# Attention into soft MoE on one core: routing matmuls moved to another place of the turn, a row pitch of 72, a shared beacon setup

## The chip, the cores and the metric

The kernel runs on one core of a Trainium2 chip. The metric is device time in microseconds (us) of one execution, smaller being better. Executions of this kernel scatter more than its profile suggests: 43 runs of the unchanged kernel on one chip lay between 235.8 and 248.6 us. A run is called fast when it is within 1.5% of the fastest run of the same kernel, else slow. With one core there is no second die to compare with, and the scatter turned out to be continuous, so beside the ratio of fast runs I give medians or means over all runs of the same rounds where they matter, and say which is which. A verdict (faster, same, slower at 2%, or unclear) rests on fast runs alone.

## The reference, cut to what matters

```python
# q, k, v: (8, 8, 576, 64); beacon_k, beacon_v: (8, 8, 16, 64)
k_all = np.concatenate([beacon_k, k], axis=2)
v_all = np.concatenate([beacon_v, v], axis=2)
a = softmax(causal(scale * q @ k_all.T))          # shortened
x = (a @ v_all).transpose(0, 2, 1, 3).reshape(4608, 512)
logits = x @ phi                                   # 32 slots
d = softmax(logits, axis=0); c = softmax(logits, axis=1)
slot_input = d.T @ x
slot_out = relu(slot_input @ w1[e]) @ w2[e]        # 8 experts, 4 slots each
out = c @ slot_out
```

## The kernel before

A turn n of the main loop scores one pair of heads and attends the pair before it. Four steps of scores go through two PSUM tiles, sc0 and sc1. Transposes and routing matmuls share two PSUM buffers of the tag tr; there is no third one.

```python
ps_tr = ctx.enter_context(tc.tile_pool(name="ps_tr", bufs=2, space=PSUM))
vh = [const.tile([P, NCH, H, DD], F16, name=f"vh{i}") for i in range(2)]   # DD = 65
...
def logit_piece(b):
    lp = ps_tr.tile([P, NCH, NSL], FP, name="tr", tag="tr")
    ...                                            # 20 matmuls xT x phi
    nc.scalar.activation(dT[b][:, :, :], lp[:, :, :], AF.Exp)
    nc.vector.memset(dT[b][0:Nb, 0, :], 0.0)
...                                                # el_piece, si_piece: 20 matmuls each, too
for n in range(NP + 1):
    score(n, 0)
    if n >= 2:
        xt_piece(n - 2)          # x^T: one tr buffer, copied out by VectorE
    score(n, 1)
    transp(n + 1)                # q, then k: two tr buffers, copied out by VectorE
    ...
    if n >= 5:                   # logits, eL, slot inputs, or nothing: one tr buffer
        br, gr = divmod(n - 5, H // 2)
        (logit_piece, el_piece, si_piece, lambda b_: None)[gr](br)
    attend(n - 1, 0)
    score(n, 2)
    attend(n - 1, 1)
    score(n, 3)
    load_pair(n + 5)
    ...                          # V of the next batch: load, cast
    while wl < min(24, (n - 3) * 2 // 3):
        load_w(wl)               # a half of an expert's weights, on POOL's queue
        wl += 1
```

The softmax here doesn't subtract the row's maximum and nothing guards it: scores larger than these inputs give would overflow.

## Time and profile before

| | before |
|---|---|
| median of three runs | 240.89 us (240.24 to 241.42) |
| span of the profile | 233.8 us |
| busy: PE, DVE, ACT, POOL | 71%, 60%, 52%, 38% |
| loop, from the first exponential of turn 5 to that of turn 31 | 34.30 to 161.75 us |
| last weight load landed | 204.33 us |
| DMA row (busy share of the 16 DMA engines) | nine tenths or more from 6 to 140 us |

The profile fell on a quick execution: 235.7 us, while the timed ones were at 241. I return to what this hid. The length of a turn is read from the timeline, as the distance of the first exponentials (128x1024) of two turns.

### The profile page before, as it was taken

The numbers are of one execution on the slowest core, as the hardware profiler recorded it, in microseconds if no ns is written. First come the engines' busy times: TensorE is split into PE (matmuls) and PEld (weight loads), VectorE is DVE, ScalarE is ACT, GpSimd is POOL, SyncE is SP. The second block draws the span as 40 slices with busy tenths as digits, with TensorE's granted clock in tenths as the row PEclk, the third lists the DMA queues.
The fourth block names the chain that finished last, engine by engine and source line by source line (L and its number), as shares of the span: only waits on it lengthen the run. The fifth ranks groups of instructions, "written<-read, shape, count | busy, mean of one in ns | idle before, by whom it ended". The sixth has DMA issues, their size and how long they took to land.

```text
span 233.8 us, 8459 instructions
## 1 busy us (share of the span) xinstructions
PE 165.9 (71%) x3728; PEld 119.0 (51%) x3728; DVE 139.1 (60%) x303; ACT 122.7 (52%) x164; POOL 87.7 (38%) x162
## 2 busy tenths in 40 slices
PE   0579988887878888788777878888589530488400
PEld 0457766666666666666555666666455310223100
DVE  4575786876767777788564778866572000059700
ACT  2085687677757668758564875877201000059600
POOL 5082444654346363565334436535824200000000
PEclk9999999999979999999997999999955555559955
DMA  6999999999999999999999996537799999829996
GB/s 212 229 297 282 296 238 268 282 250 197 265 298 266 268 248 217 263 307 250 229 256 281 263 279 114 98 47 123 110 195 207 211 207 209 143 111 424 409 422 251
DMA packets 63716, 55.66 MB, mean 238 GB/s; under 512 B 41920, under 2 KB 50112, under 8 KB 62656
## 3 DMA queue, kind: packets, MB, share of 16 engines
q1 hardware_dynamic: 50880, 38.35, 57.2%
q0 software_dynamic: 12800, 16.78, 42.4%
q8 instruction: 29, 0.48, 0.9%
q14 instruction: 7, 0.06, 0.1%
HBM read 62.46 MB, written 9.44 MB: 308 GB/s over the span
## 4 chain that ended last, share of the span: by engine, by line
PE 46%; DVE 18%; DMA 11%; ACT 10%; issue 5%; SPq 4%; POOL 0%; DVEq 0%; POOLq 0%
DMA w2h<-in_moe_w_dram 9%; ACT ex L206 7%; PE sc_154 L200 7%; PE tr L185 6%; PE av_150 L227 6%; PE tr L253 6%; PE sc_155 L200 5%; PE fp L407 3%; DVE qT_129 L187 3%; DVE qT_130 L187 3%; DVE xb_141 L235 3%; DVE qT_128 L187 3%; SPq L103 2%; PE tr L371 2%; PE av_151 L227 2%
## 5 line engine op out<-in xcount | busy, mean ns | idle before, releaser
L206 ACT ACTIVATE ex<-sc_154 128x1024 f16<-128x1024 f32 x64 | 62.9, 983 | 46.8 <-PE sc_154 L200 46.7
L208 POOL TENSOR_SCALAR_AFFINE_SELECT ex<-ex 128x1024 f16<-128x1024 f16 x32 | 34.8, 1088 | 80.3 <-ACT ex L206 80.3
L206 ACT ACTIVATE ex<-sc_155 128x992 f16<-128x992 f32 x64 | 48.2, 753 | 2.3 <-PE sc_155 L200 2.3
L227 PEld LDWEIGHTS <-ex 128*128 128x128 f16 (+2 forms) x960 | 38.6, 110 | 8.6 <-issue 7.5
L257 DVE COPY xT<-tr 128x592 f16<-128x592 f16 x32 | 14.9, 466 | 12.8 <-PE tr L253 12.8
L371 PE MATMUL tr<-siT,w1h 128*128 128x4 f16 x256 | 8.2, 167 | 13.8 <-DMA w1h<-in_moe_w_dram 13.0
L185 PE MATMUL tr<-idb,qf 64*64 64x64 bf16 x576 | 16.3, 202 | 1.5 <-PE sc_155 L200 0.8
L185 PE MATMUL tr<-idb,kf 64*64 64x64 bf16 x576 | 15.6, 199 | 2.3 <-DVE qT_130 L187 1.2
L374 ACT ACTIVATE hTz<-tr 128x32 f16<-128x32 f32 x8 | 1.6, 197 | 29.5 <-PE tr L371 29.5
L371 PEld LDWEIGHTS <-w1h 128*128 128x128 f16 x256 | 7.5, 104 | 18.1 <-DMA w1h<-in_moe_w_dram 14.2
L185 PEld LDWEIGHTS <-qf 64*64 64x64 bf16 x576 | 12.6, 115 | 7.8 <-issue 7.3
L185 PEld LDWEIGHTS <-kf 64*64 64x64 bf16 x576 | 12.8, 114 | 2.8 <-issue 1.8
L411 DVE TENSOR_SCALAR osb<-fp,rc 128x512 f32<-128x512 f32 x18 | 12.7, 748 | 2.2 <-PE fp L407 1.8
L120 POOL DMA_DIRECT2D w2h<-in_moe_w_dram x16 | 12.0, 756 | 5.0 <-PE tr L371 2.6
L407 PE MATMUL fp<-soh,eLh 128*128 128x512 f16 x36 | 12.1, 452 | 2.4 <-ACT soh L396 1.1
L120 POOL DMA_DIRECT2D w1h<-in_moe_w_dram x16 | 11.5, 722 | 5.7 <-PE tr L371 4.5
L409 ACT ACTIVATE osb<-fp,rc 128x512 f32<-128x512 f32 x18 | 11.9, 686 | 2.0 <-PE fp L407 1.6
L394 DVE TENSOR_SCALAR soh<-av_150,rd 128x256 f16<-128x256 f32 x1 | 0.5, 484 | 20.4 <-PE av_150 L388 20.4
L227 PE MATMUL av_151<-vh_137,ex 128*128 128x65 f16 (+2 forms) x240 | 11.9, 207 | 0.0
L187 DVE COPY qT_129<-tr 128x576 bf16<-128x576 bf16 x11 | 8.3, 758 | 5.9 <-PE tr L185 5.9
L227 PE MATMUL av_151<-vh_138,ex 128*128 128x65 f16 (+2 forms) x240 | 11.3, 201 | 0.5 <-issue 0.5
L227 PE MATMUL av_150<-vh_137,ex 128*128 128x65 f16 (+2 forms) x240 | 11.4, 203 | 0.0
(204 smaller groups left out, 302.8 us busy)
## 6 DMA issues: line engine op xcount, KB each, us to landing
qf<-in_q_dram SPq DMA_DIRECT2D x32, 288.0 KB, 6.3
kf<-in_k_dram SPq DMA_DIRECT2D x32, 288.0 KB, 6.3
w1h<-in_moe_w_dram POOLq DMA_DIRECT2D x16, 512.0 KB, 8.7
w2h<-in_moe_w_dram POOLq DMA_DIRECT2D x16, 512.0 KB, 9.8
out_dram<-osb SPq DMA_DIRECT2D x8, 1024.0 KB, 8.1
vf<-in_v_dram SPq DMA_DIRECT2D x24, 256.0 KB, 7.5
vf<-in_v_dram SPq DMA_DIRECT2D x8, 224.0 KB, 7.3
vf<-in_v_dram SPq DMA_DIRECT2D x8, 160.0 KB, 7.1
```

The source lines that it names most:

```text
L120: nc.gpsimd.dma_start(out=d[e][:, o:o + 2048].rearrange("p (c f) -> p c f", c=c), in_=src)
L185: nc.tensor.transpose(tp[po:po + 64, j, :], hi, idb[po:po + 64, po:po + 64])
L187: nc.vector.tensor_copy(out=dst[:, Nb:Nb + S].rearrange("p (s j) -> p s j", j=J), in_=tp[:, :, :].rearrange("p j s -> p s j"))
L200: nc.tensor.matmul(sc[0:kn, a, col:col + un], kT[n % 3][64 * a:64 * a + 64, P * c:P * c + kn], qT[n % 3][64 * a:64 * a + 64, u0:u0 + un], ...
L206: nc.scalar.activation(ex[n][:, :, o:o + w], sc[:, :, 0:w], AF.Exp, scale=scale)
L208: nc.gpsimd.affine_select(out=ex[n][:, :, 0:512].rearrange("p a (c t) -> p a c t", c=4), in_=ex[n][:, :, 0:512].rearrange("p a (c t) -> p ...
L227: nc.tensor.matmul(avs[a][0:m, i * DD:(i + 1) * DD], ex[n][0:kn, a, o:o + m], vh[b % 2][0:kn, c, h, :], start=(c == 0), stop=(c == i))
L253: nc.tensor.transpose(tp[:, P * i:P * i + m], xb[b % 2][0:m, i, 2 * g:2 * g + 2, :].rearrange("p h d -> p (h d)"), idh[0:m, 0:m])
L257: nc.vector.tensor_copy(out=xT[:, g, 0:U], in_=tp[:, 0:U])
L371: nc.tensor.matmul(hp[:, t, :], w1h[e][:, c * F + t * P:c * F + (t + 1) * P], siT[:, c, e * SPE:(e + 1) * SPE], start=(c == 0), stop=(c == ...
L407: nc.tensor.matmul(fp_[:, :], etok(cg, j), soh[:, :], start=True, stop=True)
L411: nc.vector.tensor_scalar(out=osb[:, j, :], in0=fp_[:, :], scalar1=rc[:, i:i + 1], scalar2=None, op0=AL.mult)
```

## The change

The intent was to take the routing matmuls out from between the q/k transposes and attention, where they wait for a tr buffer (0.56 us at 80.81 in the profile before); to give V and the attention outputs a row pitch of 72 for alignment; and to start the first scores earlier. `beacon_keys` is the last line of `transp`, made a function of its own.

```diff
+    DP = 72
-    nc.vector.tensor_copy(out=idh[:, :], in_=idb[:, :])
-    vh = [const.tile([P, NCH, H, DD], F16, name=f"vh{i}") for i in range(2)]
+    vh = [const.tile([P, NCH, H, DP], F16, name=f"vh{i}") for i in range(2)]
 ... (beacons: half of each copy)
-        for r in range(2):
-            nc.vector.tensor_copy(out=bkd[:, :, r, :], in_=bkf[:, :, :])
+        nc.vector.tensor_copy(out=bkd[:, :, 0, :], in_=bkf[:, :, :])
+        nc.scalar.activation(bkd[:, :, 1, :], bkf[:, :, :], AF.Copy)
 ... (attend)
-                    avs[a][0:m, i * DD:(i + 1) * DD],
+                    avs[a][0:m, i * DP:i * DP + DD + a],
-                    vh[b % 2][0:kn, c, h, :],
+                    vh[b % 2][0:kn, c, h, 0:DD + a],
 ... (start)
-    beacons()
     transp(0)
+    beacons()
+    beacon_keys(0)
+    nc.vector.tensor_copy(out=idh[:, :], in_=idb[:, :])
 ... (loop)
             score(n, 0)
+        if n >= 6:
+            br, gr = divmod(n - 6, H // 2)
+            (logit_piece, el_piece, si_piece, lambda b_: None)[gr](br)
         if n >= 2:
             xt_piece(n - 2)
 ...
-        if n >= 5:
-            br, gr = divmod(n - 5, H // 2)
-            (logit_piece, el_piece, si_piece, lambda b_: None)[gr](br)
```

More of the change, by code (lines that the diff above doesn't have):

```diff
@@ L145 @@
         nc.vector.memset(qT[i][:, 0:Nb], 0.0)
-    vh = [const.tile([P, NCH, H, DD], F16, name=f"vh{i}") for i in range(2)]
+    vh = [const.tile([P, NCH, H, DP], F16, name=f"vh{i}") for i in range(2)]
     for i in range(2):
-        nc.gpsimd.memset(vh[i][:, :, :, D:DD], 1.0)
+        nc.gpsimd.memset(vh[i][:, :, :, D:DP], 1.0)
     xb = [const.tile([P, NCH, H, D], F16, name=f"xb{i}") for i in range(2)]
@@ L158 @@
     for a_ in avs:
-        nc.vector.memset(a_[64:P, 4 * DD:5 * DD], 1.0)
+        nc.vector.memset(a_[64:P, 4 * DP:5 * DP], 1.0)
     scs = [ps_sc.tile([P, 2, 512], FP, name=f"sc{i}") for i in range(2)]
@@ L171, in beacons @@
         for r in range(2):
-            nc.vector.tensor_copy(
-                out=bkT[64 * r:64 * r + 64, :, :],
-                in_=tp[64 * r:64 * r + 64, :, :].rearrange(
-                    "p b (g r n) -> p (b g) r n", g=H // 2, r=2)[:, :, r, :])
+            dst = bkT[64 * r:64 * r + 64, :, :]
+            src = tp[64 * r:64 * r + 64, :, :].rearrange(
+                "p b (g r n) -> p (b g) r n", g=H // 2, r=2)[:, :, r, :]
+            if r == 0:
+                nc.vector.tensor_copy(out=dst, in_=src)
+            else:
+                nc.scalar.activation(dst, src, AF.Copy)
     def transp(n):
@@ L189, in transp, with beacon_keys @@
                 in_=tp[:, :, :].rearrange("p j s -> p s j"))
+        if n > 0:
+            beacon_keys(n)
+    def beacon_keys(n):
         nc.gpsimd.tensor_copy(out=kT[n % 3][:, 0:Nb], in_=bkT[:, n, :])
@@ L227, in attend @@
                 nc.tensor.matmul(
-                    avs[a][0:m, i * DD:(i + 1) * DD],
+                    avs[a][0:m, i * DP:i * DP + DD + a],
                     ex[n][0:kn, a, o:o + m],
-                    vh[b % 2][0:kn, c, h, :],
+                    vh[b % 2][0:kn, c, h, 0:DD + a],
                     start=(c == 0), stop=(c == i))
         r5 = sml.tile([P, NCH], FP, name="r5", tag="r5")
-        avv = avs[a][:, 0:NCH * DD].rearrange("p (i d) -> p i d", d=DD)
+        avv = avs[a][:, 0:NCH * DP].rearrange("p (i d) -> p i d", d=DP)
         nc.vector.reciprocal(out=r5[:, :], in_=avv[:, :, D])
@@ L288, in si_piece @@
                                 op=AL.add)
+    transp(0)
     beacons()
-    transp(0)
+    beacon_keys(0)
+    nc.vector.tensor_copy(out=idh[:, :], in_=idb[:, :])
     wl = 0
```

## The prediction

> **What bounds the kernel now.** I read the page first, then the waits, then the timeline of a few turns of the attention loop, then the DMA rows. No engine is full on the page (PE 71%, DVE 60%, ACT 52%), so the limit has to be a chain or DMA. The waits, busiest first, do not name it, because POOL's and ACT's idle time is only slack. The timeline does. This is one turn of the loop (one pair of heads) that also carries a routing piece, from the timeline, columns start, duration, engine, line, what, count, and the idle time before with its releaser:
>
> ```profile
> 79.14 0.41 PE L200 MATMUL sc_155<-qT_130,kT_133 64*80 64x80 bf16 x6
> 79.48 0.47 PE L185 MATMUL tr<-idb,qf 64*64 64x64 bf16 x18
> 79.79 0.45 PE L185 MATMUL tr<-idb,kf 64*64 64x64 bf16 x18
> ...
> 80.00 0.76 DVE L187 COPY qT_128<-tr 128x576 bf16<-128x576 bf16 x1 [0.28 <-PE tr L185]
> ...
> 80.81 0.45 PE L274 MATMUL tr<-idh,dT 128*32 128x128 f16 x20 [0.56 <-DVE qT_128 L187]
> ...
> 81.19 0.67 PE L227 MATMUL av_150<-vh_138,ex 128*128 128x65 f16 x15
> ...
> 81.78 0.37 PE L200 MATMUL sc_154<-qT_130,kT_133 64*128 64x464 bf16 x2
> ...
> 82.20 0.94 ACT L206 ACTIVATE ex<-sc_154 128x928 f16<-128x928 f32 x1 [1.37 <-PE sc_154 L200]
> ...
> 83.19 0.40 PE L200 MATMUL sc_154<-qT_128,kT_131 64*128 64x128 bf16 x8 [0.24 <-ACT ex L206]
> ```
>
> The reader is to see that the routing transposes (L274) stand between the q/k transposes and attention. They need one of the two buffers of tag tr, and both hold transposes that VectorE has not yet copied out. TensorE runs in order, so attention behind them waits too: 0.56 us idle and 0.38 us of own work (80.81 to 81.19). Then the third score step, its exponential (0.94) and the next first score step follow in series. The chain that ended last goes through exactly these places:
>
> ```profile
> 80.00 0.77 DVE qT_128 L187
> 80.77 0.04 issue
> 80.81 0.45 PE tr L274 x20
> 81.25 0.60 PE av_150 L227 x15
> 81.85 0.32 PE sc_154 L200 x2
> 82.17 0.02 issue
> 82.20 0.95 ACT ex L206
> ```
>
> The starts of the first exponential give the length of four consecutive turns: 73.84, 78.91, 83.71, 88.61, 92.40, that is 5.07 (logits), 4.80 (eL), 4.90 (slot inputs), 3.79 (no piece); sum 18.56. A piece costs about 1.1 us although its matmuls are 0.45 to 0.65 us.
>
> The second limit is DMA:
>
> ```profile
> DMA  6999999999999999999999996537799999829996
> vf<-in_v_dram SPq DMA_DIRECT2D x24, 256.0 KB, 7.5
> w2h<-in_moe_w_dram POOLq DMA_DIRECT2D x16, 512.0 KB, 9.8
> 184.33 20.01 DMA w2h<-in_moe_w_dram
> ```
>
> The row is full until slice 24 (140 us), half empty while the loop ends, and full again to 204 us. The last line, of the chain, is the final weight load, 20 us from issue to landing. So the tail is a queue of weight loads, and it starts when the loop ends, because POOL issues the rest of them in program order after the loop.
>
> [...]attention at 81.19 follows the blocked piece though its own operands were ready. [...]the 15 attention matmuls took 1.06 us at 22.98 and 0.67 at 81.19, and the granted clock over 120 to 140 us was 0.91, with a dip after idle gaps. [...]I give the V cast (0.42 us on DVE with pitch 65) no gain from pitch 72, and no run here shows it yet. [...]the identity copy of L139 took 2.12 us beside a POOL memset of 2.02 us.
>
> **The change part by part.**
>
> 1. Routing before the x^T transposes. The order of TensorE in a turn becomes: first score step, piece, x^T, second score step, q, k, attention; a piece starts one turn later (n-6 for n-5). The piece's buffer was last held by a q transpose of the turn before, long copied. It is now the q transposes that wait for the piece's copy. For eL: with the first score step at 0, the piece runs 0.38 to 0.83, its copy (0.45) ends near 1.35, while q's turn comes at 0.83 + 0.36 + 0.34 = 1.55. For logits ScalarE empties it behind the first exponential: 0.52 + 0.92 + 0.30 = 1.74 against q at 1.70; a touch at most. So the idle 0.56 goes and no new wait takes its place. The piece also covers the time in which x^T waits for the attention output (0.15 at 83.57). The turn from the start of the first score step: q at 1.09 + piece, attention 0.69 later, third score step 0.60 later, its exponential 0.42 later, next turn 0.99 later: 3.79 + piece. With pieces of 0.62, 0.45, 0.62: 4.41, 4.24, 4.41. The turn without a piece is 3.95, since VectorE's outputs still hold x^T by 0.16. Sum 17.0 against 18.56: 1.5 us for four turns, 0.5 per piece. 20 of the 21 pieces in the loop get it (the last now lies in the closing turn): 10.1 us.
>
> 2. The tail follows the end of the loop one for one, since DMA idles in 140 to 165 us. So most of the 10 us should reach the end.
>
> 3. What DMA takes back, an estimate from the landings in the trace: in the closing queue a weight load lands every 2.5 us (186.7, 189.2, 191.8), q/k loads follow each other by about 0.75, V loads by about 1.0. Four turns need 8 q/k, 5 V, 2.67 weight loads: 6 + 5 + 6.7 = 17.7 us. That is below 18.56, but above 17.0. V is the tightest: its last chunk of one batch landed at 109.60 and was cast at 109.72; others had 2 to 5 us. With unbroken turns DMA would give back 0.7 per four turns, 3.5 over five batches. But the loop also has gaps (turns of 5.6 to 6.9 near 120 to 130) in which DMA catches up. I take 2 us.
>
> 4. Setup. q/k transposes go ahead of the beacons, and ScalarE takes half of the beacon copies. The first score matmul was at 10.70. Now the beacon path is load at 6.15, copy 0.45, transposes 1.0, copy 0.5, POOL 0.2: about 8.8, 1.9 us earlier. But the third pair's k landed only at 16.66, and PE waited for it at 16.71 (0.69). That load depends on SP's queue, not on the beacons. So of 1.9 us I count 0.2.
>
> 5. Pitch 72, one column more for odd heads. Matmuls of 65 columns are spaced 40 ns (0.60 / 15), and their weight loads take 0.56 of the 0.60, so row pitch and a 66th column (240 x 2 times under 1 ns) are nothing: 0 to +0.3 us. The wider POOL memset at the start has slack until 8.99. Zero.
>
> Sum: -10.1 + 2 - 0.2 + 0.3 = about -8.0; 240.9 - 8.0 = 232.9.
>
> **The rivals.** (a) DMA is the true bound of the loop: the row stands at nine all through it. Then only 18.56 - 17.7 = 0.9 per four turns comes, about 5 over the loop, and late V casts stop POOL or VectorE: 236 to 238. Against it: SP waits for TensorE's transposes, not the other way round (39.2 us in 18 waits), and there is no DMA wait on PE after 16.71. (b) ScalarE or VectorE becomes the bound: for ScalarE 3.3 busy of 4.4 us, and for VectorE 3.9; a wait of q for logits' ScalarE copy would cost up to 0.2 for 7 pieces, 1.4 us: 234. (c) The denser TensorE keeps its clock: the dips to half clock near 67 and 125 us each follow an idle stretch and make turns of 6 us and more; fewer of them would give 2 to 4 us: 229 to 231. (d) The pitch slows or speeds attention: its 960 matmuls at 5 ns either way would be 5 us, but weight loads cover them.
>
> **Range and chances.** Most likely 233.0. High side, (a) with an unlucky dip: 237.5. Low side, (c): 229. Same needs over 236.1, that is under 4.8 us of the 10 kept: 0.16. Slower needs a new stall that I can't see: 0.02.
>
> **What would show it.** In the timeline no idle time ahead of the routing matmuls, and attention right behind k's transposes; turns near 4.3 with pieces and 3.9 without; loop end near 158 instead of 168; the last weight landing near 195 instead of 204. Wrong would be: POOL or VectorE casts that wait for V loads, q transposes that wait for ScalarE or VectorE, an earlier first score with nothing after it, or attention matmuls of another duration.

## The result, and the profile after

The changed kernel took 233.95 us (median of 4 runs, 232.28 to 237.88) against 241.15 for the one before (median of 4, 240.24 to 243.53). The ratio is 0.9685, 95% interval 0.9588 to 0.9783. A ratio is the mean time of one kernel's fast runs over that of the other's of the same rounds, so not quite the ratio of the medians. The predicted time was 233.0 in a range of 229.0 to 237.5.

The same kind of turn as in the prediction, one with an eL piece, in the timeline of the changed kernel (start, duration, engine, line, what, count, idle time before with its releaser):

```profile
81.13 0.40 PE L207 MATMUL sc_153<-qT_127,kT_130 64*128 64x128 bf16 x8 [0.24 <-ACT ex L213]
...
81.46 0.45 PE L281 MATMUL tr<-idh,dT 128*32 128x128 f16 x20
...
81.65 1.02 ACT L213 ACTIVATE ex<-sc_153 128x1024 f16<-128x1024 f32 x1 [0.16 <-PE sc_153 L207]
...
81.84 0.43 PE L260 MATMUL tr<-idh,xb_141 128*128 128x128 f16 x5
...
82.54 0.47 PE L188 MATMUL tr<-idb,qf 64*64 64x64 bf16 x18
...
82.85 0.47 PE L188 MATMUL tr<-idb,kf 64*64 64x64 bf16 x18
...
83.25 0.67 PE L234 MATMUL av_149<-vh_137,ex 128*128 128x65 f16 x15
...
84.15 0.67 PE L234 MATMUL av_150<-vh_137,ex 128*128 128x66 f16 x15
...
84.26 0.94 ACT L213 ACTIVATE ex<-sc_153 128x928 f16<-128x928 f32 x1 [0.61 <-PE sc_153 L207]
...
85.78 1.02 ACT L213 ACTIVATE ex<-sc_153 128x1024 f16<-128x1024 f32 x1 [0.16 <-PE sc_153 L207]
```

The routing transposes (L281) start without a wait, and attention (L234) stands right behind the k transposes. The first exponentials of this turn and the next began at 81.65 and 85.78, so the turn took 4.13 us, where the same turn of the kernel before took 4.80 (78.91 to 83.71). So the mechanism is there. But the loop as a whole, from the first exponential of turn 5 to that of turn 31, went from 127.45 us only to 123.36, not by the predicted 10. The missing part is in long turns. The first of them stands near 30 us, just ahead of turn 5 (28.39 to 35.01, 6.62 us, where the kernel before took 3.96); it costs time, but it is not in these two figures:

```profile
29.86 1.00 DVE L248 CAST vh_137<-vf 128x512 f16<-128x512 f32 x1 [1.50 <-DMA vf<-in_v_dram]
...
30.78 0.45 DVE L264 COPY xT<-tr 128x592 f16<-128x592 f16 x1
...
31.28 0.48 PE L188 MATMUL tr<-idb,kf 64*64 64x64 bf16 x18 [1.69 <-DVE xT L264]
...
31.69 0.98 PE L234 MATMUL av_149<-vh_136,ex 128*128 128x65 f16 x15
```

VectorE waits for a V load, x^T's copy stands behind it in VectorE's order, and the k transposes wait for the buffer that this copy frees. Then 15 attention matmuls take 0.98 us instead of 0.67: the array has fallen to half clock (on record from 31.82 to 35.24). The rows of the two pages show that half clock came more often in the changed kernel's profile (kernel before first):

```profile
PEclk9999999999979999999997999999955555559955
DMA  6999999999999999999999996537799999829996
```

```profile
PEclk9999979979999999689995999999965555569955
DMA  6999999999999999999999998828799999839996
```

Each digit is one fortieth of the span. Summed from the clock records between the first exponentials of turns 5 and 31, the profile before had 6.8 us at half clock, the one after 17.3 us. In these turns of the changed kernel no cast waited for a V load. What stands in the long ones is TensorE time without a named releaser, called "issue" in the waits (engine, line, what it waited for, total us, times, longest): 5.5 us in all, against 2.2 us in the kernel before. Of the changed kernel:

```profile
PE tr L188 <- issue: 3.9, 5, 1.5
...
PE av_149 L234 <- issue: 0.9, 1, 0.9
...
PE sc_154 L207 <- issue: 0.6, 1, 0.6
```

The longest of them in the timeline, and the attention matmuls behind it at half clock:

```profile
93.72 0.26 PE L188 MATMUL tr<-idb,kf 64*64 64x64 bf16 x2 [1.46 <-issue]
93.91 1.06 PE L234 MATMUL av_149<-vh_136,ex 128*128 128x65 f16 x15
```

The three stretches of half clock that begin in turns 5 to 31 of this profile, and the two of the profile before, each begin during such a wait or within 2.6 us of its end. In the profile before, for one, a wait of 0.97 us ended at 125.51, and the next 15 attention matmuls took 1.04 us instead of 0.67.

So the question for the experiments was not whether the order works, but what took half of it back.

### The profile page after: what moved, and what is told of

Its sections match the earlier page's. It is cut to its first block, busy times and chain, and to the rows that moved or that the text cites. A ratio compares the mean times of both kernels' runs of the same rounds, so it can differ in the third digit from the quotient of the medians.

```text
span 230.2 us, 8457 instructions
## 1 busy us (share of the span) xinstructions
PE 169.1 (73%) x3728; PEld 121.2 (53%) x3728; DVE 134.9 (59%) x301; ACT 124.5 (54%) x166; POOL 88.5 (38%) x162
## 3 DMA queue, kind: packets, MB, share of 16 engines
q0 software_dynamic: 12800, 16.78, 42.6%
## 4 chain that ended last, share of the span: by engine, by line
PE 43%; DMA 19%; ACT 13%; issue 6%; DVE 5%; SPq 4%; POOL 2%; DVEq 0%; ACTq 0%; POOLq 0%
DMA w2h<-in_moe_w_dram 15%; PE tr L188 10%; ACT ex L213 10%; PE sc_153 L207 8%; PE av_149 L234 8%; PE sc_154 L207 4%; PE tr L260 4%; SPq L104 3%; PE fp L416 3%; DMA vf<-in_v_dram 3%; ACT osb L418 2%; PE av_150 L234 2%; PE tr L290 2%; DMA qf<-in_q_dram 2%; PE tr L281 1%
## 5 line engine op out<-in xcount | busy, mean ns | idle before, releaser
L234 PEld LDWEIGHTS <-ex 128*128 128x128 f16 (+2 forms) x960 | 39.3, 111 | 9.8 <-issue 8.3
L188 PE MATMUL tr<-idb,qf 64*64 64x64 bf16 x576 | 17.0, 205 | 7.7 <-DMA qf<-in_q_dram 5.1
L188 PEld LDWEIGHTS <-qf 64*64 64x64 bf16 x576 | 13.8, 117 | 14.1 <-issue 8.0
L188 PE MATMUL tr<-idb,kf 64*64 64x64 bf16 x576 | 16.9, 202 | 5.3 <-issue 3.0
L188 PEld LDWEIGHTS <-kf 64*64 64x64 bf16 x576 | 14.2, 117 | 6.8 <-issue 5.5
L416 PE MATMUL fp<-soh,eLh 128*128 128x512 f16 x36 | 11.6, 428 | 2.5 <-ACT soh L405 1.1
L190 DVE COPY qT_127<-tr 128x576 bf16<-128x576 bf16 x11 | 8.3, 757 | 7.5 <-PE tr L188 7.4
L234 PE MATMUL av_149<-vh_137,ex 128*128 128x65 f16 (+2 forms) x240 | 11.7, 203 | 0.9 <-issue 0.9
L207 PEld LDWEIGHTS <-kT_131 64*128 64x128 bf16 (+1 forms) x198 | 7.9, 101 | 8.2 <-issue 5.7
L190 DVE COPY qT_128<-tr 128x576 bf16<-128x576 bf16 x11 | 8.3, 758 | 6.3 <-PE tr L188 6.2
```

What stands on the lines that cost most here:

```text
L188: nc.tensor.transpose(tp[po:po + 64, j, :], hi, idb[po:po + 64, po:po + 64])
L190: nc.vector.tensor_copy(out=dst[:, Nb:Nb + S].rearrange("p (s j) -> p s j", j=J), in_=tp[:, :, :].rearrange("p j s -> p s j"))
L207: nc.tensor.matmul(sc[0:kn, a, col:col + un], kT[n % 3][64 * a:64 * a + 64, P * c:P * c + kn], qT[n % 3][64 * a:64 * a + 64, u0:u0 + un], ...
L234: nc.tensor.matmul(avs[a][0:m, i * DP:i * DP + DD + a], ex[n][0:kn, a, o:o + m], vh[b % 2][0:kn, c, h, 0:DD + a], start=(c == 0), stop=(c ...
L416: nc.tensor.matmul(fp_[:, :], etok(cg, j), soh[:, :], start=True, stop=True)
```

## The experiments

Three theories stood. **A**: the order gives some 10 us, and DMA takes a good part of it back, since the loop now runs as fast as its loads. **B**: the order gives less than its clean turns show, and setup or pitch, perhaps through an earlier full clock (a granted clock of 1.00 is first on record at 26.52 us in the profile before, at 21.58 in the one after), carries part of the gain. **C**: the long turns and the half clock come by themselves, without DMA.

All runs were in groups that shared one chip and the runs of the kernel before. Means are over all runs, slow ones too, with 95% intervals of the difference (normal; for rows of six runs they should be 5 to 25% wider). The verdicts, from fast runs: r1_order, p1_pitch, o1_order_setup and s1b_setup are "same"; a1_after and the other rows with a ratio are "unclear"; s1_setup and n1_before_nov, with one fast run each, have none.

| run | runs | median us | mean minus mean of before | ratio of fast runs |
|---|---|---|---|---|
| chip 1: before | 43 | 240.82 | | |
| r1_order | 22 | 237.70 | -2.1 ± 1.2 | 0.996 (0.992 to 1.001) |
| p1_pitch | 23 | 240.66 | +0.4 ± 1.4 | 1.004 (0.999 to 1.010) |
| s1_setup | 6 | 244.47 | +3.2 ± 2.3 | none given |
| a1_after | 6 | 236.00 | -3.7 ± 2.1 | 0.988 (0.973 to 1.003) |
| chip 2: before | 11 | 242.49 | | |
| n1_before_nov | 6 | 231.58 | -11.2 ± 2.4 | none given |
| n2_after_nov | 6 | 225.18 | -17.6 ± 2.3 | 0.928 (0.915 to 0.941) |
| w1_late_weights | 6 | 232.47 | -9.4 ± 2.1 | 0.971 (0.962 to 0.979) |
| b2_after_attend | 6 | 232.13 | -9.9 ± 2.3 | 0.963 (0.954 to 0.972) |
| chip 3: before | 43 | 241.86 | | |
| n3_before_qk | 6 | 272.49 | +31.1 ± 1.3 | 1.146 (1.139 to 1.153) |
| n4_after_qk | 6 | 261.82 | +19.9 ± 1.2 | 1.101 (1.093 to 1.108) |
| o1_order_setup | 22 | 238.34 | -3.3 ± 1.4 | 0.994 (0.989 to 0.998) |
| s1b_setup | 22 | 240.47 | -1.3 ± 1.2 | 1.003 (0.997 to 1.008) |

### r1_order, p1_pitch, s1_setup, a1_after: the parts

r1_order is the kernel before with only the loop part of the diff; p1_pitch has only the lines with DP; s1_setup has only the setup lines; a1_after is the changed kernel again.

```diff
 # r1_order
             score(n, 0)
+        if n >= 6:
+            br, gr = divmod(n - 6, H // 2)
+            (logit_piece, el_piece, si_piece, lambda b_: None)[gr](br)
         if n >= 2:
             xt_piece(n - 2)
 ...
-        if n >= 5:
-            ...
```

> The kernel before with the new place of the routing piece alone (ahead of x^T, one turn later); pitch and setup stay old. Theory (the piece no longer waits for a tr buffer): nearly the whole gain, ratio to before 0.970 (0.960 to 0.980). Rival (setup, by an earlier start and an earlier full clock, carries the gain): over 0.985. In the profile no idle time of about 0.56 us ahead of the routing matmuls; turns of four pairs sum to about 17.1 us instead of 18.56 where the clock is full.

> The kernel before with pitch 72 alone (and 66 columns for odd heads). Theory: nothing, ratio 0.995 to 1.005, V cast still 0.42 us on VectorE and 0.61 on POOL, 15 attention matmuls still spaced 0.60 us. Rival (alignment helps the moving reads or the casts): below 0.99.

> The kernel before with the new setup alone (q and k transposes first, ScalarE shares the beacon copies, identity copy later). Theory: first score matmul about 1.5 us earlier, but the third pair of loads holds it again: ratio 0.993 to 1.001. Rival[...]: 0.98 to 0.99.

> The changed kernel again, in the rounds of its parts: 0.97 of before. If parts add, the product of the three others' ratios equals this within 0.006.

Pitch did nothing, as expected: +0.4 ± 1.4 us; with full clock 15 attention matmuls took 0.67 us with pitch 65 and with pitch 72, and the V cast on VectorE 0.42 us with both (14 of the 16 casts in the profiles before and after). The order alone gained, but much less than expected, 2.1 us by means and nothing clear by fast runs; its ratio fell on the rival's side of the mark (over 0.985), so setup had to be tested again (below). In its profile (a slow run) the routing matmuls no longer waited for a tr buffer and clean turns were the same as in the changed kernel, yet the turn ahead of turn 5 took 10.1 us, for the reason seen above (timeline, same columns), and in turns 5 to 31 TensorE stood 10.1 us in waits without a releaser:

```profile
32.59 0.43 DVE L241 CAST vh<-vf 128x512 f16<-128x512 f32 x1 [5.39 <-DMA vf<-in_v_dram]
...
33.45 0.69 PE L185 MATMUL tr<-idb,kf 64*64 64x64 bf16 x18 [5.01 <-DVE xT L257]
...
35.23 0.61 POOL L241 CAST vh<-vf 80x512 f16<-80x512 f32 x1 [5.28 <-DMA vf<-in_v_dram]
```

The changed kernel gained 3.7 ± 2.1 us here, about half of the 7.2 of the first comparison (four runs each), and its ratio of 0.988 missed the expected 0.97; where the true gain lies these runs don't say. The test of whether the parts' ratios multiply could not be made, since s1_setup got no ratio; the means of the three parts sum to +1.5 us with it, and to -3.0 with its repeat below on another chip. The setup alone was slower in its first six runs; I repeated it below.

### n1_before_nov and n2_after_nov: most V loads taken away

Wrong results on purpose: V is loaded for the first batch and used for all. Same instructions on the engines otherwise.

```diff
     def load_v(b, part):
         for c in ((0, 1), (2,), (3,), (4,))[part]:
+            if b > 0:
+                vf[(b, c)] = vf[(0, c)]
+                continue
```

> The kernel before, but V is loaded for the first batch only and used for all (wrong result on purpose, same instructions otherwise): the largest part of the DMA pressure of the loop is gone. Theory (DMA takes back half of what the new order gives): the long turns go, 5 to 8 us off before, since clean turns stay at 18.56 for four. Rival (the lost gain is the clock or the chip's scatter alone): under 3 us.

> The changed kernel with V of the first batch alone (wrong on purpose). Theory: now the order gives its full 9 to 10 us against the same cut of before: 10 to 15 us off the changed kernel's 236, and turns of 17.1 for four nearly everywhere. Rival: the distance between the two cut kernels stays at about 5 us as between the whole ones.

The kernel before fell by 11 us, more than expected: it, too, had lost time to DMA, which its quick profile had hidden. The distance of the two cut kernels was 6.4 us in the medians (also in the means, 230.9 and 224.5). That is nearer to the rival's 5 than to the 9 to 10 of the theory. The changed one's profile (a slow run) still had 10.2 us of half clock in the loop and 3.9 us of waits without a releaser. Weight loads were still in the loop, so I went further.

### n3_before_qk and n4_after_qk: no V loads, and no weight loads in the loop

```diff
-        while wl < min(24, (n - 3) * 2 // 3):
+        while wl < 0:
```

in addition to the edit above, in both kernels; all 32 weight loads then queue behind the loop, which makes the end later but is the same for both.

> The kernel before with V of the first batch alone (wrong on purpose) and no weight load until the loop is over: in the loop DMA moves q and k alone, some 6 us of work for four turns of 18.56. Its end is later, since all 32 weight loads queue behind the loop, so it is read from its turns. Theory: nearly all turns clean (5.07, 4.80, 4.90, 3.79), loop some 121 us from turn 5 to turn 31. Rival (the long turns come from the instruction fetch or the clock by themselves): long turns and half clock as before.

> The changed kernel with the same cuts (wrong on purpose). Theory: turns of 4.71, 4.13, 4.24, 3.95 nearly everywhere, loop some 111 us from turn 5 to turn 31, and the medians of the two cut kernels 8 to 10.5 us apart, the whole clean gain. Rival: 5 to 6.5 apart, as with V alone taken away.

This settled how much the order gives. All twelve runs were fast, within 2.6 us of each other for either kernel, and the medians are 10.67 us apart (ratio of the two means 0.959). The turns from 5 to 31 were clean throughout: 5.07, 4.80, 4.90, 3.78 in the cut kernel before and 4.71, 4.12, 4.24, 3.95 in the cut changed one, each within about 0.02 from batch to batch, and 121.2 against 110.8 us in all. The clock stood at full speed in the whole loop of both. Busy time of the engines (PE, PEld, DVE, ACT, POOL, each with its number of instructions) from 35 to 140 us, with the granted clock, the DMA share (the packets' time over that of 16 engines; above 1 where packets overlap) and GB/s as the last three columns, first of the cut kernel before and then of the cut changed one:

```profile
35.00:140.00 105.00, 88.87 (x2370) 68.52 (x2369) 80.48 (x185) 75.36 (x96) 43.69 (x85) 1.00 0.40 122
```

```profile
35.00:140.00 105.00, 96.80 (x2554) 74.36 (x2553) 83.42 (x203) 83.31 (x107) 47.36 (x93) 1.00 0.40 121
```

The kernels with all their loads, over 35 to 137 us, had this (before, then after):

```profile
35.00:137.00 102.00, 84.16 (x2163) 64.85 (x2162) 73.53 (x171) 68.71 (x89) 49.76 (x92) 0.97 1.12 259
```

```profile
35.00:137.00 102.00, 89.72 (x2194) 68.77 (x2194) 72.47 (x172) 71.72 (x91) 50.13 (x92) 0.92 1.10 258
```

With the DMA share at 0.40 the clock is 1.00 and TensorE does 2370 matmuls in the one kernel and 2554 in the other, 8% more in the same time. With the share at 1.1 and the bytes per second equal (259 and 258), the changed kernel finishes 2194 instead of 2163, 1.4% more. That the loads take the gain back is theory A, and it is shown. That the loop runs exactly as fast as its loads is not: SyncE's q and k loads still waited for TensorE's q and k transposes, 37.0 us in 18 waits in the changed kernel and 39.2 in the one before, so each waits for the other. Theory C falls: stalls and half clock went away with the loads, with the engines' other instructions unchanged. (The cut does not part V from weights, nor the bytes from the 0.72 to 0.76 us that POOL spends on issuing each weight load. The two kernels also differ in setup and pitch, but the 10.4 us are between turns 5 and 31.)

How the loads do it the waits' lists don't say, but the traces do. The waits of TensorE without a named releaser were absent from both cut kernels. The DMA table has a queue that carries instructions, in every profile with the same 29 packets; in the changed kernel's:

```profile
q8 instruction: 29, 0.48, 0.9%
```

The packets are of 16384 bytes each, and their times are in the packed traces, though no view prints them one by one. In the twelve profiles with weight loads left in the loop TensorE has 83 waits of over 0.2 us without a releaser, the longest 2.8 us. Every one ends 1.2 to 1.8 us after the end of a packet of this queue, and the record behind the wait (TensorE's matmuls, weight loads and sequencer records, counted from 0) is number 256n + 193, 194 or 195, with n the packets that had come by then. From these two coincidences I conclude that TensorE stood there for its own next 256 instructions; no view of the profile names it. In turns 5 to 31 these waits sum to 2.2 us in the profile before, 5.5 after, 10.8 in o1_order_setup and 10.8 in w1_late_weights (all fast runs), and none in n3 and n4. A late V load, by contrast, held TensorE for over 1 us once per profile at most: in turn 4 of eight profiles and in turn 8 of s1b_setup. Why the packets come late beside the loads is open; they are not longer than in the cut kernels (0.9 to 1.7 us in the loop in these four profiles, 0.9 to 2.1 in n3 and n4).

### o1_order_setup and s1b_setup: what setup and pitch do beside the order

o1_order_setup is the changed kernel with DP = DD and no 66th column; s1b_setup is s1_setup once more.

> The changed kernel with the old pitch of 65 (order and setup new). Theory: pitch does nothing, so within 0.5% of the changed kernel, about 0.98 of before. If the pitch carries part of the gain (the changed kernel had a lower mean than the order alone by 1.6 us): within 0.5% of the order alone, 0.99.

> The setup alone once more, since six runs of it had a mean 3.2 us above before. If that was scatter: within 1 us of before. If the earlier start does cost with the old order: 2 to 4 us above again.

Setup alone is now 1.3 ± 1.2 us quicker, so the 3.2 us of loss before was not reproduced. I take setup as a microsecond either way; its sign is open. o1_order_setup, at -3.3 ± 1.4 us on this chip, is like the whole change on chip 1 (-3.7 ± 2.1), so the pitch carries nothing that these runs can see. Theory B falls, up to that microsecond. But the expectation had set 0.98 against 0.99 for a pitch that matters, and the fast-run ratio came out at 0.994 (the means give 0.986): the fast rule picks the quickest runs of each kernel, and the kernel before, with 43 runs, has a few very quick ones. As the changed kernel did not run on this chip, the case against the pitch rests on p1_pitch.

### w1_late_weights and b2_after_attend: using what was learned

If the end is a queue of weight loads and DMA is less busy at the end of the loop (share 0.68 over 140 to 165 us in the changed kernel's profile, against 1.10 over 35 to 137), weights should be issued there, and faster. w1_late_weights is the changed kernel with:

```diff
-        while wl < min(24, (n - 3) * 2 // 3):
+        while wl < min(24, max((n - 3) * 2 // 3, 2 * n - 36)):
```

b2_after_attend adds to it: the piece moves behind the second attention of the turn (n-5), where TensorE waits for an exponential anyway (0.24 us at 85.26 in the changed kernel's profile; 25 such waits there, 6.5 us in all), and the small memset of logit_piece goes to POOL.

```diff
-        nc.vector.memset(dT[b][0:Nb, 0, :], 0.0)
+        nc.gpsimd.memset(dT[b][0:Nb, 0, :], 0.0)
-        if n >= 6:                     # ahead of xt_piece
-            ...
             attend(n - 1, 1)
+        if n >= 5:
+            br, gr = divmod(n - 5, H // 2)
+            (logit_piece, el_piece, si_piece, lambda b_: None)[gr](br)
```

> The changed kernel with the same weight loads, but two a turn from turn 26 on, so that all 24 that fit are issued by the last turn instead of 18, in the time in which the DMA row is half empty. Theory (a queue of weight loads behind the loop sets the end): six loads of 2.5 us leave the closing queue, 8 to 14 us off the changed kernel. Rival (TensorE's half clock or the experts' matmuls set the tail): under 4 us.

> As w1_late_weights, with the piece behind the second attention of its turn (n-5) where TensorE waits for the exponential anyway, and the small memset of the logits on POOL so that x^T's copy does not wait for ScalarE. If turns were bound by the chain, 16.1 for four instead of 17.0, 5 us below w1. If DMA bounds the loop by now (estimate 17.7), within 2 us of w1.

w1_late_weights gave a correct result and 232.47 us, 9.4 ± 2.1 below before; the changed kernel was 3.7 below on another chip. So it beats the kernel before; against the change it gains 5.7 ± 3.0 us, by an inference across two chips through before, and only about 2 if the first comparison's 7.2 us is taken. In its profile 36.7 us pass from the first exponential of the last turn to the landing of the last weight load (162.33 to 198.99), against 42.6 in the changed kernel (158.37 to 201.00): 6 us, not the expected 8 to 14. The reason is in POOL's timeline:

```profile
160.21 1.50 POOL L121 DMA_DIRECT2D w2h<-in_moe_w_dram  x2
...
173.91 1.43 POOL L121 DMA_DIRECT2D w1h<-in_moe_w_dram  x2 [8.77 <-PE tr L380]
```

All 24 loads for which there is room are out at 161.7, but the other eight need the buffers of the first experts, and these are read only after the routing tail. The queue runs dry in between (its last load landed at 172.8).

b2_after_attend shortened the clean turns again, to 4.14, 3.8 and less, and its time is that of w1 within 0.6 us in the means. In its profile (a slow run) turns of 6 to 8 us stood beside the short ones, and TensorE's waits without a releaser were 17.1 us in turns 5 to 31, against 10.8 in w1's (a fast run, so this is a hint only). The expectation had 5 us less than w1 if the chain on TensorE were the bound, and the same time within 2 us if DMA were; the second came.

## Why the prediction was right, point by point

The order's mechanism and its clean gain were right; the step that failed is part 3, what DMA takes back, in its size and in the way it happens.

- **The order (part 1).** Right. Four turns were predicted at 17.0 instead of 18.56; the cut kernels show 17.02. The gain by the order was put at 10.1 us; with V and weight loads out of the way it was 10.4 us in the loop and 10.67 in the medians. (Its own figures, 18.56 - 17.0 over three pieces, give 10.4 for 20 pieces; and q's turn in its eL sum is at 1.53, not 1.55.) The single turns were less exact: 4.41, 4.24, 4.41, 3.95 predicted; 4.71, 4.12, 4.24, 3.95 measured. The logits turn is longer because the memset on VectorE waits for ScalarE's exponential and holds x^T's copy behind it, which the prediction named only as "a touch at most". In the timeline of the changed kernel:

```profile
78.21 0.47 PE L188 MATMUL tr<-idb,qf 64*64 64x64 bf16 x18 [0.25 <-ACT dT L273]
...
78.22 0.07 DVE L274 MEMSET dT<- 16x16 uint32 x1 [1.83 <-ACT dT L273]
78.22 0.45 DVE L264 COPY xT<-tr 128x592 f16<-128x592 f16 x1
```

- **The tail (part 2).** Right that it follows the loop one for one: in the two profiles the last turn came 3.4 us earlier and the last weight load landed 3.3 us earlier. The times named for it did not come (loop end near 158, last landing near 195): the loop's last attention ended at 163.1 and the last load landed at 201.0, since the loop itself had gained so little in this profile.
- **What DMA takes back (part 3).** The step that failed in size: 2 us were put down, and at most 3.5. The full gain is 10.67 us, and the whole kernels differed by 7.2 us in the first comparison, by 3.7 ± 2.1 on chip 1, and by 3.3 ± 1.4 on chip 3 (there without the pitch). So DMA took 3.5 to 7 us. The step counted how much longer the transfers take than the turns, 17.7 us against 17.0. What the runs showed in its place is TensorE waiting for its own instructions beside the loads: 5.5 us in turns 5 to 31 of the changed kernel's profile and 10.8 with old pitch (2.2 before), with half clock behind the waits (17.3 us against 6.8), and none of either without V and weight loads. To this comes, ahead of turn 5, a V load that reaches TensorE through VectorE's queue (6.62 us for a turn of 3.96), which the prediction had named as a sign of being wrong. How the lost time splits between these waits, the half clock and the late V load is not worked out. The step also started from a profile of before that happened to be quick; the idle stretches ahead of the dips near 67 and 125 us, which it saw, were such waits for instructions (0.74 and 0.97 us). Its point that no DMA wait was left on TensorE after 16.71 holds for the loop's data alone (in the tail TensorE waited 13.0 us for w1h).
- **Setup (part 4).** Counted at 0.2 us; measured between -1.3 ± 1.2 and +3.2 ± 2.3. The first score matmul came at 9.20 instead of 10.70 (8.8 had been worked out, though its five terms sum to 8.3), and TensorE then stood at the third pair's q load, as said of that pair's k load:

```profile
15.13 0.69 PE L188 MATMUL tr<-idb,qf 64*64 64x64 bf16 x18 [1.23 <-DMA qf<-in_q_dram]
```

- **Pitch (part 5).** Right: nothing. That the V cast would gain nothing was an estimate that no run had shown; p1_pitch came out so.
- **The rivals.** (a), DMA as the bound, was the right one to fear; it holds in part (for the V casts ahead of turn 5, and through the instructions, which it did not foresee), and on chips 1 and 3 the changed kernel's median (236.0, and 238.3 without the pitch) was in or just above the time that it foresaw. (b) happened in the small: five to seven waits of up to 0.25 us. (c) went the other way in the profile on record: 17.3 us of half clock in turns 5 to 31, not less than 6.8. (d) did not happen.

The time came out within 1 us of the prediction in the first comparison. That is partly luck: on the two other chips the gain was about half, 236 to 238 us, near the upper end of the range, and the verdicts there were "unclear" and (without the pitch) "same".

## What to carry to other kernels

When an engine stands before a buffer that another engine must first copy out, and the work behind it waits too (as attention did here, behind 0.56 us idle at 80.81), put the work with the late buffer where its buffer has long been free; count the clean turns from the timeline (here the sum of four came out within 0.2%, single turns within 7%). Before adding such gains up, work out how long the transfers of a turn take; here, with the new turns shorter than that, a third to two thirds of the gain was kept. The loads need not hold the engine directly (in the changed kernel's profile TensorE had 5.5 us of waits without a releaser in turns 5 to 31, and none with V and weight loads cut): look at its waits without a releaser, and whether they stand 256 instructions or a multiple of it apart. To separate the two, take the loads away in both kernels: here the scatter shrank with them, to 2.5 us over six runs, where six runs with more loads spread over 4.8 to 7.6.
